# Projections spread over two bursts, and blocks that begin as soon as their tokens are split, in a two-layer attention kernel

## Chip, cores and metric

The kernel runs on one core of one Trainium2 chip. The metric is the device time of one execution in microseconds, the median of several runs.

## The reference

Four blocks run one after the other over 2048 tokens of width 576, in fp32: A, B, A, B, each on a layer norm of its input, each added to it. A is attention with 32 query heads of width 18 that share one key and one value head; B is linear attention with learned features. Both layers use the same weights.

```python
def _A_ref(x, wq, wk, wv, wo):
    q = (x @ wq).reshape(B, S, H, Dh).transpose(0, 2, 1, 3)
    k, v = x @ wk, x @ wv
    scores = jnp.einsum("bhqd,bkd->bhqk", q, k) * (Dh ** -0.5)
    o = jnp.einsum("bhqk,bkd->bhqd", _softmax(scores), v)
    return o.transpose(0, 2, 1, 3).reshape(B, S, H * Dh) @ wo

def _B_ref(x, wqkv, w_phi, wo):
    q, k, v = ...            # x @ wqkv, by heads
    pq = jnp.einsum("bhsd,hdf->bhsf", q, w_phi)      # pk likewise from k
    phi_q = concat([_softmax(pq), _softmax(-pq)])    # phi_k likewise
    kv = jnp.einsum("bhsf,bhsd->bhfd", phi_k, v)
    z = jnp.einsum("bhsf->bhf", phi_k)
    o = (phi_q @ kv) / (phi_q @ z + 1e-6)
    return o.transpose(0, 2, 1, 3).reshape(B, S, D) @ wo

x = x + _A_ref(_layernorm(x), ...)
x = x + _B_ref(_layernorm(x), ...)
# and both once more
```

## The kernel before

A layer here is A followed by B. Nearly all its time goes to one loop in `attend`, which computes A's attention and, in the gaps, most of B's projections for those token tiles whose attention is already finished. There are 16 token tiles of 128 tokens. A group is one token tile with half of the heads, so there are 32 groups; a unit is one group, one key tile and half of the group's heads, so a loop has 1024 units.

For each unit TensorE (PE) makes two score products into one of three score tiles `sc` (line 572), ScalarE (ACT) takes their exponential into a tile `pt` (line 1044), and PE later adds both units of a key tile into the group's sums, four products per key tile (line 850; "a key tile of sums" below). The sums of a group stand in one of two banks of PSUM, `acc` and `ps`, which change roles from group to group; the bank that is free takes the projections. When a group's last key tile is added, `finish_group` turns, divides and splits its sums on VectorE (DVE) and writes them to DRAM.

The loop goes in bursts of `BURST` = 3 units (`burst`). A burst issues the scores of three units and then does one of two things. Either it fills the free bank with one bankful of projections (`fill`), 14 products of 288 columns (`project`, line 257); or it adds key tiles of sums, two or three (`count`), and may add a state update (`U`, line 649) after them. A bankful costs one credit; `earn` gives `st["pace"]` credits per three units, and a burst with a bankful is followed by one without (`paused`). Where the side work has nothing to do (`st["idle"]`), two units and one key tile go at a time.

The side work is the generator `stream`. For each token tile it makes the output projection of finished attention (`output`, two bankfuls with the weights `wd`) and a block `mix`: keys (two bankfuls, `wa`), values (two, `wb`), queries (two, `wc`) and the state update. DVE takes each bankful out of PSUM (copies at lines 605 and 636) and makes the features. Eight bankfuls and one update go with each token tile, that is with 64 units.

The next tile's tokens are made ready beside that: layer norm in place on DVE (line 711), a block transpose on DVE (line 700), a write to DRAM (`flipped`, line 705) and a load back, turned (`xn`, lines 718 and 720); `turn_tokens` then splits them into high and low parts `xs` (lines 134, 135, 726, 727) once the previous block's update is issued. `turn_next` is asked after each bankful of a block: once it makes the statistics, the next time the turning. A block begins when `wanted` says so.

PE and DVE instructions of the loop are held in the order in which this code writes them (`in_order`), so what is written before what decides who waits.

Of the kernel before, what the change touches and what calls it, by code (L numbers as in the profile page):

```python
# [19 lines left out]
P = 128  # L20
# [4 lines left out]
NT = S // P  # L25
# [32 lines left out]
def traced(nc):  # L58
    return nc.cur_bb.bb.instructions
# [3 lines left out]
def kernel(ctx, tc, x_in, wq, wk, wv, wo, wqkv, w_phi, wob, out):  # L63
# [87 lines left out]
    def weight_tiles(place):  # L151
        hi = wpool.tile([P, KT, D], F32R, name=f"w{place}hi")
        return hi, (Parts("wclo") if place == "c" else wpool.tile([P, KT, D], F32R, name=f"w{place}lo"))
# [405 lines left out]
    def load_shifts(dst, layer, c, g):  # L559
        for j in range(2):  # L560
            src = mxds[layer][:, g * HG + j * HG // 2 : g * HG + (j + 1) * HG // 2, tokens(c)]
            to = dst[j * ROWT + KEYS : j * ROWT + STK].bitcast(F32)
            nc.sync.dma_start(to.rearrange("r p (x t) -> r (p x) t", t=P), src)
# [360 lines left out]
    def attend(layer, st, a1o, stream):  # L924
# [7 lines left out]
        def fetch(n):  # L932
            c, g = groups[n]
            qst[c, g] = a1.tile([P, 2, CW], F32R, name="qst")
            load_queries(qst[c, g], layer, c, g)
            load_shifts(qst[c, g], layer, c, g)

        with ctx1:
# [53 lines left out]
            def tick():  # L992
                ticks[0] += 1
                for queue in (urgent, loads, slow):
                    begun = len(traced(nc))
                    if queue and next(queue[0], DONE) is DONE:
                        queue.popleft()
                    if queue is loads:
                        for i in traced(nc)[begun:]:
                            if i.engine == mybir.EngineType.SP:  # L1000
                                tc.add_manual_dep(i, last[PE], SYNC if loads_at[0] is None else NOSYNC, reason="order")
                                loads_at[0] = i.name

            kind, credit, paused = [None], [0.0], [False]

            def peek():
                while kind[0] is None and bulk:
                    v = next(bulk[0], DONE)
                    if v is DONE:
                        bulk.popleft()  # L1010
                    elif v is STAGE:
                        break
                    elif isinstance(v, Kind):
                        kind[0] = v
                return kind[0]

            def fill():
                kind[0] = None
                while True:
                    v = next(bulk[0])  # L1020
                    assert v is not STAGE
                    if v < 0:
                        break
                in_order()

            last = {}

            def in_order():
                for i in traced(nc)[mark[0] :]:
                    if i.engine in PINNED:  # L1030
                        if i.engine in last:
                            tc.add_manual_dep(i, last[i.engine], NOSYNC, reason="order")
                        last[i.engine] = i.name
                mark[0] = len(traced(nc))
# [3 lines left out]
            pts, at, done = {}, [0], [0]  # L1038

            def expose(n, t, hh, pt):  # L1040
                sc = pss.tile([P, 2, 512], F32, name="sc")
                for j in range(2):
                    score(sc[:, j, :], qst[groups[n]], 2 * hh + j, t)
                A.activation(pt, sc, AF.Exp, scale=SCALE)  # L1044
                pts[n, t, hh] = pt

            spots = [*st["head"], *(a1.tile([P, 2, 512], F32, name="pt", bufs=TILES) for _ in range(2 * BURST))]
            acc[groups[0]] = bank(*homes[0], [P, CW])
            at[0] = len(spots)
            done[0] = (at[0] - 2 * BURST) // 2  # L1050

            def head_values(t, first, last):
                add_values(acc[groups[0]], t, [pts[0, t, j // 2][:, j % 2, :] for j in range(GH)], first, last)

            def head():
                for n, (unit, pt) in enumerate(zip(units, spots)):
                    expose(*unit, pt)
                    t = n // 2 - BURST
                    if n % 2 and t >= 0:
                        head_values(t, t == 0, False)  # L1060
# [6 lines left out]
            with tc.If(nc.values_load(safe[0:1, 0:1], min_val=0, max_val=1) == 0):  # L1067
# [5 lines left out]
                for g in range(2):  # L1073
                    load_shifts(st[f"q{g}"], layer, 0, g)
                head_values(BURST - 1, False, True)
                head()
# [6 lines left out]
            def scores(count):  # L1083
                ready = at[0] // 2
                for n, t, hh in units[at[0] : at[0] + count]:
                    if t == 0 and hh == 0 and 0 < n < len(groups) - 1:
                        fetch(n + 1)
                    expose(n, t, hh, a1.tile([P, 2, 512], F32, name="pt", bufs=TILES))
                    at[0] += 1
                in_order()  # L1090
                return ready

            def sums(until):
                while done[0] < until:
                    n, t, _ = units[2 * done[0]]
                    values(*groups[n], t, [pts.pop((n, t, hh)) for hh in range(2)])
                    done[0] += 1
                    in_order()

            def earn(count):  # L1100
                credit[0] = min(credit[0] + st["pace"] * count / BURST, 2)

            def burst():
                ready = scores(BURST)
                tick()
                earn(BURST)
                work = peek()
                held = at[0] + BURST - 2 * done[0]
                if work == "P" and credit[0] >= 1 and not paused[0] and held <= TILES:
                    fill()  # L1110
                    credit[0] -= 1
                    paused[0] = True
                else:
                    paused[0] = False
                    count = 3 if credit[0] + st["pace"] >= 1 else 2
                    until = min(ready, max(done[0] + count, -(-(at[0] + BURST - TILES) // 2)))
                    opens = any(t % NT == 0 for t in range(done[0], until))
                    if work == "F" and credit[0] >= 1 and not opens:
                        fill()
                        credit[0] -= 1  # L1120
                    sums(until)
                    if work == "U":
                        fill()
                    tick()
# [17 lines left out]
                run(gen)  # L1142

    BURST = 3
    TILES = 9
    DUE = 9
    SPILL = 4
    SETTLE = 3
    PACES = ((0.6, 0.39), (0.39, 0.39))
    FLIP = 84  # L1150
    TAIL = 100
    KEPT = NT - 3
    PE = mybir.EngineType.PE
    PINNED = (PE, mybir.EngineType.DVE)
# [17 lines left out]
    st = {"late": [], "norms": const.tile([P, NT // PAIR], F32, name="norms"), "wq": weight_tiles("b")}  # L1172
# [8 lines left out]
    def bank(pool, tag, shape):  # L1181
        t = pool.tile([P, CW], F32, name=tag)[: shape[0]]
        if len(shape) == 2:
            return t[:, : shape[1]]
        return t[:, : shape[1] * shape[2]].rearrange("p (a b) -> p a b", b=shape[2])
# [89 lines left out]
    for layer in range(LAYERS):  # L1275
        last = layer == LAYERS - 1
        st.update(start_state(bw), added=set())
        with tc.tile_pool(name="a1o", bufs=2) as a1o:

            def load(key, place, *args, **kw):  # L1280
                st[key] = weight_tiles(place) if isinstance(place, str) else place.weights()
                yield from reload_weight(key) if key in wd else load_weight(st[key], *args, **kw)
# [7 lines left out]
            def stream(v, layer=layer):  # L1290
                ps, loads, slow, finished, ticks = v.ps, v.loads, v.slow, v.finished, v.ticks
                residual = x_in.rearrange("(i p) d -> i p d", p=P) if layer == 0 else xd
                held, spoiled = deque(maxlen=3), set()
                unflipped, st["left"] = deque(), list(range(NT))
                st["closed"], st["pace"] = -1, PACES[layer][0]

# [41 lines left out]
                else:  # L1338
                    loads.append(load_wv())
                    loads.append(load("wk", "a", scratch[1], slice(0, D), padded=True))  # L1340
                    loads.append(load("wpq", "c", scratch[0], slice(0, D), padded=True))
                st["pace"] = PACES[layer][1]
                fetched = xs = None
                weights = False

                settled = 0
# [6 lines left out]
                        settled = v.left() - SETTLE  # L1353

                def wanted():
                    return (xs is not None and xs[0] != KEPT and v.left() <= settled
                            and (xs[0] < st["closed"] or xs[0] == NT - 2 or v.left() < TAIL))

                def flip(i, stats):
                    nonlocal fetched  # L1360
# [28 lines left out]
                while v.left():  # L1389
# [21 lines left out]
                    elif wanted():  # L1411
# [4 lines left out]
                        xs = None  # L1416
# [11 lines left out]

            st["heads_in"] = lambda: a1o.tile([P, 9, P], F32R, name="on", bufs=1)
            attend(layer, st, a1o, stream)  # L1430

            psx = ExitStack()
# [8 lines left out]
            with tc.tile_pool(name=f"tail{layer}", bufs=1) as tail:  # L1441
# [11 lines left out]
                xs = bw.tile([P, 9, P], F32R, name="xs2")  # L1453
# [115 lines left out]
```

## Time and profile before

| | |
|---|---|
| runs, us | 2678.7, 2674.51, 2678.91 (median 2678.7) |
| profiled execution, us | 2673.21 |
| its span, us | 2671.4 |
| mean granted PE clock | 0.993 |
| busy in the span: PE, DVE, ACT | 97%, 47%, 81% |

The span of an execution runs from its first to its last instruction. In a stretch of a timeline or a table, times are microseconds from the span's start; "PEld" is PE's load of weights, which runs beside its products. A row of the timeline gives start, length, engine, line, operation, output and inputs, the count, and in brackets how long the engine was idle before and who ended that. A table by stretch gives its bounds and length, the busy time of each engine with its count of instructions, the granted clock, the busy share of the DMA engines and GB/s. Products of fp32 sums (line 850) count twice in the profile, 24 rows for three key tiles.

### The profile page before, as it was taken

Reading aid. Unit: us, or ns where it says so; the run is one execution under the profiler, and the core shown is the slowest. Engines: PE = TensorE matmul, PEld = TensorE weight load, DVE = VectorE, ACT = ScalarE, POOL = GpSimd, SP = SyncE. Lnnn points to the kernel's source line nnn. Section 1 sums busy time; section 2 is a strip of 40 time slices with the busy share of each in tenths; the row PEclk is TensorE's granted clock in tenths of the full one; section 3 lists DMA queues with packets and bytes.
Section 4 is the critical chain, followed back from the end, with each engine's and each line's share of the span. In section 5 each row is a group of like instructions: output and inputs, shape, how many; then the busy total and the mean of one; then the engine's idle time right before and its main releaser. Section 6 shows DMA issues by size and latency. Waiting matters only on the chain. (4 is left out here: it accounts for less than half of the span.)

```text
span 2671.4 us, 55505 instructions
## 1 busy us (share of the span) xinstructions
PE 2597.6 (97%) x22002; PEld 1439.7 (54%) x22002; DVE 1266.8 (47%) x2871; ACT 2154.2 (81%) x2529; POOL 66.0 (2%) x106
## 2 busy tenths in 40 slices
PE   7989999999999999999999999999999999999999
PEld 6633444444444444438996344444444444444498
DVE  8444455444444444436774424444444444444265
ACT  4578989999999999994334999999999999999821
POOL 1000000000000000002000000000000000000010
PEclk9999999999999999999999999999999999999999
DMA  5465243222222222225643322222222222222164
GB/s 185 141 158 150 73 132 95 60 60 60 60 60 59 55 56 57 59 66 159 187 153 111 99 55 55 60 60 60 60 60 60 60 60 59 54 55 56 47 195 141
DMA packets 491633, 232.95 MB, mean 87 GB/s; under 512 B 237734, under 2 KB 458214, under 8 KB 491366
## 3 DMA queue, kind: packets, MB, share of 16 engines
q1 hardware_dynamic: 489894, 226.37, 31.4%
q8 instruction: 176, 2.88, 0.5%
q10 hardware_dynamic: 1472, 2.95, 0.4%
q14 instruction: 91, 0.75, 0.1%
HBM read 130.62 MB, written 96.67 MB: 85 GB/s over the span
## 5 line engine op out<-in xcount | busy, mean ns | idle before, releaser
L1044 ACT ACTIVATE pt<-sc 128x1024 f32<-128x1024 f32 x2036 | 1923.2, 1054 | 180.6 <-PE sc L572 158.9
L572 PE MATMUL sc<-qst,kst 56*128 56x512 f32 x3840 | 699.6, 452 | 22.5 <-ACT pt L1044 22.1
L572 PEld LDWEIGHTS sc<-qst,kst 56*128 56x128 f32 x3840 | 319.1, 184 | 564.8 <-ACT pt L1044 515.0
L850 PE MATMUL acc<-pt,vst 128*32 128x512 f32 x4096 | 500.3, 600 | 0.0
L850 PE MATMUL ps<-pt,vst 128*32 128x512 f32 x4048 | 480.9, 598 | 2.9 <-DVE featk L605 2.9
L850 PEld LDWEIGHTS ps<-pt,vst 128*32 128x32 f32 x4048 | 109.1, 109 | 229.2 <-issue 225.1
L850 PEld LDWEIGHTS acc<-pt,vst 128*32 128x32 f32 x4096 | 103.9, 109 | 211.0 <-issue 209.4
L321 DVE TENSOR_TENSOR xc<-xc,acc 128x288 f32<-128x288 f32 x60 | 27.2, 454 | 321.8 <-PE acc L257 321.8
L257 PE MATMUL ps<-wahi,xs 128*128 128x288 f32 x693 | 150.5, 303 | 2.1 <-ACT xs L132 1.9
L257 PE MATMUL ps<-wchi,xs 128*128 128x288 f32 x576 | 127.1, 306 | 0.0
L257 PE MATMUL acc<-wdhi,on 128*128 128x288 f32 x540 | 119.8, 307 | 3.2 <-DVE xc L321 3.2
L257 PEld LDWEIGHTS ps<-wahi,xs 128*128 128x128 f32 x693 | 114.4, 190 | 6.3 <-ACT xs L132 2.6
L257 PE MATMUL ps<-walo,xs 128*128 128x288 f32 x385 | 113.3, 297 | 0.0
L605 DVE COPY featk<-acc 128x288 f32<-128x288 f32 x51 | 23.3, 458 | 182.9 <-PE acc L257 182.9
L450 PE MATMUL ps<-xsc,wbhi 128*128 128x256 f32 x576 | 107.4, 285 | 0.6 <-ACT xsc L132 0.6
L472 ACT ACTIVATE pc<-ps 128x256 fp32r<-128x256 f32 x80 | 30.4, 384 | 93.2 <-PE ps L450 91.7
L257 PEld LDWEIGHTS ps<-wchi,xs 128*128 128x128 f32 x576 | 94.0, 188 | 19.2 <-issue 18.6
L132 ACT ACTIVATE xs<-ps 128x512 fp32r<-128x512 f32 x36 | 21.4, 595 | 102.7 <-PE ps L307 102.7
L257 PE MATMUL acc<-wahi,xs 128*128 128x288 f32 x459 | 101.8, 307 | 0.0
L257 PEld LDWEIGHTS acc<-wdhi,on 128*128 128x128 f32 x540 | 88.2, 188 | 24.9 <-issue 21.2
L257 PE MATMUL ps<-wclo,xs 128*128 128x288 f32 x320 | 94.2, 295 | 0.0
L450 PEld LDWEIGHTS ps<-xsc,wbhi 128*128 128x128 f32 x576 | 91.2, 193 | 1.6 <-ACT xsc L132 1.0
(256 smaller groups left out, 3064.4 us busy)
## 6 DMA issues: line engine op xcount, KB each, us to landing
qst<-qd SPq DMA_DIRECT2D x360, 72.0 KB
od<-parts SPq DMA_DIRECT2D x512, 36.0 KB
pht<-phi SPq DMA_DIRECT2D x32, 540.0 KB
qd<-pc SPq DMA_DIRECT2D x64, 256.0 KB
on<-od SPq DMA_DIRECT2D x60, 256.0 KB
phi<-pht SPq DMA_DIRECT2D x104, 144.0 KB
xd<-xc SPq DMA_DIRECT2D x33, 288.0 KB
flipped<-pht SPq DMA_DIRECT2D x112, 72.0 KB
```

The source lines that it names most:

```text
L132: A.activation(dst_hi, src, AF.Copy)
L257: T.matmul(dst, xs[:, slot, :], w[half][:, k, c0 : c0 + HALF], start=(n == 0), stop=(n == last))
L321: V.tensor_add(xr, xr, po)
L450: T.matmul(po, lhs, xsc[:, slot, :], start=(n == 0), stop=(n == LASTP))
L472: A.activation(pc[:, 0, :], po, AF.Copy)
L572: T.matmul(sc, kst[head_rows(h), t * P : (t + 1) * P], q[head_rows(h), h // 2, :], start=True, stop=True)
L605: V.tensor_copy(e[:, hs, 0, :], src)
L850: T.matmul(acc[32 * j : 32 * j + 32, :], vst[:, t, :], pts[j], start=first, stop=last)
L1044: A.activation(pt, sc, AF.Exp, scale=SCALE)
```

## The change

`fill` can run only a part of a bankful: `PIECE` = 3 steps, six products, and the rest (eight) in a later burst. With less than one credit but at least half of one, a burst begins a bankful and pays 0.5; the rest costs 0.5 too. Bursts with sums add three key tiles instead of two already from half a credit in sight. The pace becomes 0.38 instead of 0.39. `wanted` no longer asks that a later token tile's attention is closed, so a block may begin right after its tokens are split (three units after that is issued, `SETTLE`).

```diff
-            def fill():
-                kind[0] = None
-                while True:
+            def fill(steps=None):
+                while steps != 0:
                     v = next(bulk[0])
                     assert v is not STAGE
                     if v < 0:
+                        kind[0], begun[0] = None, False
                         break
+                    if steps is not None:
+                        steps -= 1
+                        begun[0] = True
                 in_order()
...
-                if work == "P" and credit[0] >= 1 and not paused[0] and held <= TILES:
-                    fill()
-                    credit[0] -= 1
+                whole = begun[0] or credit[0] >= 1
+                part = 0.5 if begun[0] or not whole else 1
+                opens = any(t % NT == 0 for t in range(done[0], done[0] + 4))
+                if (work == "P" and credit[0] >= part and not paused[0] and held <= TILES
+                        and (whole or not opens)):
+                    fill(None if whole else PIECE)
+                    credit[0] -= part
                     paused[0] = True
                 else:
                     paused[0] = False
-                    count = 3 if credit[0] + st["pace"] >= 1 else 2
+                    count = 3 if credit[0] + st["pace"] >= 0.5 else 2
...
+    PIECE = 3
...
-    PACES = ((0.6, 0.39), (0.39, 0.39))
+    PACES = ((0.6, 0.38), (0.38, 0.38))
     FLIP = 84
-    TAIL = 100
...
                 def wanted():
-                    return (xs is not None and xs[0] != KEPT and v.left() <= settled
-                            and (xs[0] < st["closed"] or xs[0] == NT - 2 or v.left() < TAIL))
+                    return xs is not None and xs[0] != KEPT and v.left() <= settled
```

More of the change, by code (lines that the diff above doesn't have):

```diff
@@ L1002, in tick @@
                                 loads_at[0] = i.name
-            kind, credit, paused = [None], [0.0], [False]
+            kind, credit, paused, begun = [None], [0.0], [False], [False]
             def peek():
```

## The prediction

> **What bounds the kernel now.** I read the page first, then busy time by stretch for the tile `pt` alone (the exponentials on ACT and the sums that read them), then the timeline of single bursts. The page:
>
> ```profile
> span 2671.4 us, 55505 instructions
> PE 2597.6 (97%) x22002; PEld 1439.7 (54%) x22002; DVE 1266.8 (47%) x2871; ACT 2154.2 (81%) x2529; POOL 66.0 (2%) x106
> ```
>
> PE looks full and ACT nearly so. The change touches the two attention loops only, so these are cut into stretches: both loops from the end of the first state update (line 649) to the end of the last, one token block, and the idle stretch at the end.
>
> ```profile
> 331.91:1149.11 817.20, 362.05 (x3048) 82.14 (x3048) 722.50 (x762) 1.00 0.27 67
> 1636.62:2456.81 820.19, 364.39 (x3072) 82.59 (x3072) 727.68 (x768) 1.00 0.24 58
> 739.27:807.59 68.32, 30.37 (x256) 6.88 (x256) 60.65 (x64) 1.00 0.24 58
> 807.59:817.05 9.46, 5.05 (x40) 0.89 (x40) 8.86 (x10) 1.00 0.17 50
> 846.62:855.26 8.64, 5.70 (x48) 1.25 (x48) 8.44 (x10) 1.00 0.14 39
> 2490.00:2510.00 20.00, 10.99 (x92) 1.57 (x80) 19.05 (x22) 1.00 0.21 58
> ```
>
> First the length, then PE, weight loads and ACT with counts, then the clock. One block takes 68.32 us for 64 exponentials. Without projections an exponential costs 20.00 / 22 = 0.91 us; three bursts with two key tiles of sums each take 8.64 us for nine (the tenth belongs to a neighbour), 0.96 each. A projection pair is dearer:
>
> ```profile
> 823.70 0.53 PEld L572 LDWEIGHTS sc<-qst,kst 56*128 56x128 f32 x6 [0.84 <-ACT pt L1044]
> 824.31 5.80 ACT L1044 ACTIVATE pt<-sc 128x1024 f32<-128x1024 f32 x6 [0.28 <-PE sc L572]
> 824.60 0.19 PEld L257 LDWEIGHTS acc<-wahi,xs 128*128 128x128 f32 x1 [0.36 <-issue]
> ...
> 826.65 0.30 PEld L572 LDWEIGHTS sc<-qst,kst 56*128 56x128 f32 x4 [0.16 <-issue]
> 827.22 0.19 PEld L572 LDWEIGHTS sc<-qst,kst 56*128 56x128 f32 x2 [0.27 <-ACT pt L1044]
> 827.64 2.78 PE L850 MATMUL ps<-pt,vst 128*32 128x512 f32 x24
> ...
> 830.35 0.53 PEld L572 LDWEIGHTS sc<-qst,kst 56*128 56x128 f32 x6 [0.84 <-ACT pt L1044]
> ```
>
> From 823.70 to 830.35 it is three scores, 14 products, three scores, three key tiles of sums: 6.65 us for six exponentials, 1.11 each. The row to see is 827.22: even behind all 14 products the sixth score waits, because there are three score tiles and the third exponential still holds one. The sums start 0.42 us after it and last 2.71 (to 830.35); meanwhile ACT has only three scores left and runs dry. So the long sums after a full burst set the pair's length, not the products.
>
> **The split bankful.** With six products instead of 14 (14 take 826.65 - 824.60 = 2.05; about 0.13 each) the second burst's scores reach PE 1.05 us earlier; with eight, 0.79 earlier. The first exponential starts 0.61 after the first score in both, so the third ends when it did, the sixth score goes at 827.22 as before and the sums at 827.64. The products saved become a wait on PE: a pair with 6, 8 or 14 products costs 6.65 us. That is an estimate for the new pairs, since no row has one; its floor is PE's own work, 5.60 and 5.86 us.
>
> The order shows what was traded. PE inside a block, before: three bursts with two key tiles each, between two bankfuls.
>
> ```order
> L572 MATMUL sc<-qst,kst 128x512 x6
> L850 MATMUL ps<-pt,vst 32x512 x8
> L572 MATMUL sc<-qst,kst 128x512 x6
> L850 MATMUL acc<-pt,vst 32x512 x8
> L572 MATMUL sc<-qst,kst 128x512 x6
> L850 MATMUL acc<-pt,vst 32x512 x8
> ```
>
> After, inside a block of layer 2:
>
> ```order
> L572 MATMUL sc<-qst,kst 128x512 x6
> L257 MATMUL ps<-wahi,xs 128x288
> L257 MATMUL ps<-walo,xs 128x288
> L257 MATMUL ps<-wahi,xs 128x288 x2
> L257 MATMUL ps<-walo,xs 128x288
> L257 MATMUL ps<-wahi,xs 128x288
> L572 MATMUL sc<-qst,kst 128x512 x6
> L850 MATMUL acc<-pt,vst 32x512 x12
> ```
>
> The cheap double-tile bursts are gone and triple sums, which need a pair each, stand in their place. Counted over both loops in PE's order: 47 bankfuls are split, bursts ending in triple sums rise from 186 to 263 (the new limit 0.5 for three), double ones fall from 129 to 38, and one-tile steps with two scores from 142 to 95.
>
> Blocks now come as 10 pairs and an update (60 exponentials), or these and one burst with one tile and one with two (66). The update costs 807.59 - 804.31 - 2.71 = 0.57:
>
> ```profile
> 804.31 2.78 PE L850 MATMUL acc<-pt,vst 128*32 128x512 f32 x24
> ...
> 807.59 0.53 PEld L572 LDWEIGHTS sc<-qst,kst 56*128 56x128 f32 x6
> ```
>
> The short pair I price from the 9.46 us row, six tenths, 5.7. So 60 cost 67.1 and 66 cost 72.8. Layer 1 has five and seven: 845.1 for 762, where the first row has 817.2 for 762: **+28**. Layer 2 has four and seven (778.0), and a block of 84 with nine pairs, an update and 30 exponentials at the idle price (87.7): 865.7 for 786. Before: 820.2 for 768, and 18 more in the idle stretch at 0.91: 836.6. **+29**. Together **+57 us**. No wall time comes from the earlier start by itself: exponentials are fixed in number, and the stretch moves to idle bursts.
>
> **Blocks that begin at once.** Before, DVE turned the next token tile (line 711) a projection pair and more ahead of the update; row 792.43 is such a place.
>
> ```profile
> 792.43 0.57 DVE L711 TENSOR_SCALAR xc<-xc,rstd,lnb 128x576 f32<-128x576 f32 x1
> 793.85 1.99 SPq L705 DMA_DIRECT2D flipped<-pht  x4
> 797.33 0.38 SPq L718 DMA_DIRECT2D xn<-flipped  x1
> ...
> 258.65 0.58 SPq L166 DMA_DIRECT2D wstage<-folded  x1
> 262.37 0.46 DVE L134 CAST wchi<-wstage 128x576 fp32r<-128x576 f32 x1 [2.00 <-DMA wstage<-folded]
> ```
>
> Turning goes out to DRAM and back: the load is issued 4.9 us after 792.43. Its landing has no row; it lies between its issue (4.9) and the 3.7 us from issue to use of the load at 258.65 (8.6). I take 7.3, since the stores needed about 1.5 us to land (797.33 - 795.84). DVE's order around the update, before (the turning stands 15 rows above):
>
> ```order
> L609 TENSOR_TENSOR featq<-fmin,featq 128x16x18
> L610 TENSOR_TENSOR featq<-featq,fmax 128x16x18
> L655 TENSOR_TENSOR kv<-kv,ps 128x288
> L134 CAST xs<-xn 128x512
> L135 TENSOR_TENSOR xs<-xn,xs 128x512
> ```
>
> After, in layer 2:
>
> ```order
> L610 TENSOR_TENSOR featq<-featq,fmax 128x16x18
> L711 TENSOR_SCALAR xc<-xc,rstd_21664,lnb_21666 128x576
> L700 STREAM_TRANSPOSE pht<-xc 128x576
> L655 TENSOR_TENSOR kv<-kv,ps 128x288
> L134 CAST xs<-xn 128x512
> L135 TENSOR_TENSOR xs<-xn,xs 128x512
> ```
>
> The turning has slid to right before the update, so the split behind it must wait for the round trip, and the next key projections for the split. Six blocks of layer 2 stand so.
>
> ```profile
> 805.25 0.46 DVE L610 TENSOR_TENSOR featq<-featq,fmax 128x288 f32<-128x288 f32 x1
> 808.07 0.42 DVE L134 CAST xs<-xn 128x512 fp32r<-128x512 f32 x1
> 808.52 0.69 DVE L135 TENSOR_TENSOR xs<-xn,xs 128x512 fp32r<-128x512 f32 x1
> ```
>
> In this block, turning at 805.7, behind line 610, would land at 813.0, 4.9 us after 808.07. Even undelayed the split ends at 809.2, 0.5 after the third product wants it (807.59 and 0.9 of scores and two products of 0.13): 5.4 us per block, less 1.05 in the three whose first burst has six products. **+29** (15 to 37 with the ends of the landing). Queued behind on DVE are the next copies out of PSUM; on PE everything.
>
> One block before already began straight after its update:
>
> ```profile
> 331.91 0.53 PEld L572 LDWEIGHTS sc<-qst,kst 56*128 56x128 f32 x6
> 335.41 0.54 PEld L572 LDWEIGHTS sc<-qst,kst 56*128 56x128 f32 x6 [0.16 <-ACT pt L1044]
> 339.24 2.55 PE L850 MATMUL ps<-pt,vst 128*32 128x512 f32 x16 [2.86 <-DVE featk L605]
> 345.38 0.53 PEld L572 LDWEIGHTS sc<-qst,kst 56*128 56x128 f32 x6 [0.84 <-ACT pt L1044]
> ...
> 338.00:341.00 3.00, 1.76 (x16) 0.42 (x16) 2.86 (x8) 0.88 (x1) 0.00 (x0) 0.90 0.32 76
> 341.00:344.00 3.00, 3.00 (x17) 1.04 (x17) 2.41 (x4) 2.06 (x3) 0.00 (x0) 0.53 0.17 64
> 344.00:348.00 4.00, 4.00 (x38) 1.13 (x30) 0.00 (x0) 3.48 (x5) 0.00 (x0) 1.00 0.91 261
> ```
>
> A new sum bank had to wait 2.86 us for DVE's copy, because the end of an attention group stands ahead of that copy in DVE's order. The three bursts took 13.5 us against 8.7 (826.65 - 823.70 and two double-tile bursts at 2.88), **4.8** lost. In two blocks of layer 1 DVE's order is the same: **+9.5**. Nine others only meet the 0.5 us of the split: **+5**.
>
> The last rows also show the clock: after the wait of 2.86 us it was 0.53 for 3 us (0.10 and 0.47 of 3 us lost, 1.7 us). Six longer waits cost six times that, **+10**. [...]
>
> Sum: 57 + 29 + 9.5 + 5 + 10 = **110.5 us**. The profiled execution took 2673.2 (span 2671.4), so 2783.7; it lay 5.5 below the median 2678.7 of the runs, so the forecast is **2789**.
>
> **Rivals.**
> *Cover holds.* The round trip and DVE's queue hide, only the pairs cost: 2678.7 + 57 = 2736. For it: DVE is busy 47%. Against: the order leaves no instruction between turning and split that lasts 5 us.
> *Faster.* If PE alone bounds, split pairs take 5.60 and 5.86: 47 x (1.05 + 0.79) = 86 saved, 57 - 86 = -29, and if the stalls hide too, 2650. It decides where a sixth score need not wait for ACT. For it: PE's 97%. Against: row 827.22. [...]
> *Clock in every pair.* If each of the 94 half-bankful pairs' waits of 0.8 to 1.05 us halved the clock as above, 94 x 1.7 = 160 more: 2949. Against: in the stretch 807.59:817.05, whose bursts wait for ACT on PE, the clock is 1.00. [...]
> *Nothing.* The products fall as ordered, so this needs gains and losses to cancel.
>
> **How the numbers follow.** Forecast case 0.70, cover 0.19, faster 0.05, clock 0.04, nothing 0.02. The range runs from 2728, the covered case with the split pairs 0.1 us cheaper (94 x 0.1 = 9), to 2823: landing at its far end (+8), all pairs 0.1 us dearer (263 x 0.1 = 26). Faster or slower means by over 0.2%, about what a measurement of this kernel can tell: 0.05, 0.02, 0.93.
>
> **What would show it.** Right: 6.65 us for pairs with 6 and 8 products, the wait in front of their sixth score; DVE waiting some 5 us for `xn<-flipped` in six blocks of layer 2, with the clock at half behind each. Wrong: pairs under 6.2 us, or `xs` split without a wait.

## The result and the profile after

| | before | after |
|---|---|---|
| median of the runs, us | 2676.61 (4 runs, 2673.64 to 2678.91) | 2809.24 (4 runs, 2807.66 to 2812.07) |
| profiled span, us | 2671.4 | 2805.9 |
| mean granted PE clock | 0.993 | 0.984 |

The changed kernel is slower: 1.0502 times the time before, 95% interval 1.0489 to 1.0515. The medians differ by 132.6 us, the two profiled spans by 134.5. Forecast were 2789 us and a range of 2728 to 2823.

The busy times of after, then three groups of instructions, each before and after (busy time and mean; then the idle time in front of the group and who ended most of it). Lines behind the change have moved by three: the exponential, 1044 before, is 1047.

```profile
PE 2636.1 (94%) x22002; PEld 1461.3 (52%) x22002; DVE 1261.4 (45%) x2871; ACT 2149.6 (77%) x2529; POOL 66.0 (2%) x106
...
L1044 ACT ACTIVATE pt<-sc 128x1024 f32<-128x1024 f32 x2036 | 1923.2, 1054 | 180.6 <-PE sc L572 158.9
L1047 ACT ACTIVATE pt<-sc 128x1024 f32<-128x1024 f32 x2036 | 1922.2, 1052 | 312.1 <-PE sc L572 298.2
L572 PE MATMUL sc<-qst,kst 56*128 56x512 f32 x3840 | 699.6, 452 | 22.5 <-ACT pt L1044 22.1
L572 PE MATMUL sc<-qst,kst 56*128 56x512 f32 x3840 | 717.8, 454 | 69.5 <-ACT pt L1047 69.3
L257 PE MATMUL ps<-wahi,xs 128*128 128x288 f32 x693 | 150.5, 303 | 2.1 <-ACT xs L132 1.9
L257 PE MATMUL ps<-wahi,xs 128*128 128x288 f32 x882 | 201.4, 313 | 41.5 <-DVE xs L134 38.0
```

PE and ACT issue as many instructions as before, and ACT is busy as long (2154.2 us before). What has grown is waiting. ACT was idle 312.1 us in front of its exponentials, most of it waiting for scores, where it was 180.6 before. PE's scores waited 69.5 us where it was 22.5, nearly all for an exponential: that is where the split pairs show. PE waited 38.0 us for the split of tokens, where it had no such wait: the blocks that begin at once.

By stretch, from the end of the first state update to the end of the last, for tile `pt` alone (length, PE, weight loads and ACT, clock):

```profile
330.10:1195.00 864.90, 358.79 (x3048) 85.46 (x3048) 721.78 (x762) 1.00 0.25 64
1671.70:2596.40 924.70, 371.67 (x3144) 87.86 (x3144) 744.27 (x786) 0.97 0.22 53
```

The counts are the forecast's, 762 and 786 exponentials. Layer 1 took 864.9 - 817.2 = 47.7 us longer. Layer 2 took 924.7 against the 836.6 worked out for before, 88.1 longer. Together that is 135.8, so all other parts of the kernel gave back 1.3.

**A split pair.** In the timeline of PE in layer 2, pairs with six, eight and 14 products follow each other (selected rows; a row is start, length, instruction and the idle time before it):

```profile
1706.24 0.53 PEld L572 LDWEIGHTS sc<-qst,kst 56*128 56x128 f32 x6 [0.84 <-ACT pt L1047]
1708.12 0.51 PE L572 MATMUL sc<-qst,kst 56*128 56x512 f32 x2
1708.84 0.49 PE L572 MATMUL sc<-qst,kst 56*128 56x512 f32 x2 [0.21 <-ACT pt L1047]
1709.75 0.51 PE L572 MATMUL sc<-qst,kst 56*128 56x512 f32 x2 [0.42 <-ACT pt L1047]
1710.19 2.78 PE L850 MATMUL ps<-pt,vst 128*32 128x512 f32 x24
...
1712.90 0.53 PEld L572 LDWEIGHTS sc<-qst,kst 56*128 56x128 f32 x6 [0.84 <-ACT pt L1047]
1716.41 0.50 PE L572 MATMUL sc<-qst,kst 56*128 56x512 f32 x2 [0.41 <-ACT pt L1047]
1716.84 2.78 PE L850 MATMUL ps<-pt,vst 128*32 128x512 f32 x24
...
1719.56 0.53 PEld L572 LDWEIGHTS sc<-qst,kst 56*128 56x128 f32 x6 [0.84 <-ACT pt L1047]
1723.07 0.19 PEld L572 LDWEIGHTS sc<-qst,kst 56*128 56x128 f32 x2 [0.27 <-ACT pt L1047]
1723.50 2.78 PE L850 MATMUL ps<-pt,vst 128*32 128x512 f32 x24
...
1726.21 0.53 PEld L572 LDWEIGHTS sc<-qst,kst 56*128 56x128 f32 x6 [0.84 <-ACT pt L1047]
```

The pairs begin at 1706.24, 1712.90, 1719.56 and the next at 1726.21: 6.66, 6.66 and 6.65 us, whatever the products. The sixth unit's scores (the prediction's "sixth score") stand at 1709.75, 1716.41 and 1723.07, each 3.51 us behind the pair's start. With six products PE had reached the fourth unit's already at 1708.12 and then waited for ACT before the fifth and again before the sixth.

**A block that begins at once.** The timeline around an update of layer 2, with SyncE's queue (SPq) and DVE, and then the one row of PE's waits that this fills (total, times, longest):

```profile
1906.77 0.58 DVE L711 TENSOR_SCALAR xc<-xc,rstd,lnb 128x576 f32<-128x576 f32 x1
1908.19 1.99 SPq L705 DMA_DIRECT2D flipped<-pht  x4
1908.73 0.53 PEld L572 LDWEIGHTS sc<-qst,kst 56*128 56x128 f32 x6
1911.78 0.38 SPq L718 DMA_DIRECT2D xn<-flipped  x1
1914.79 0.43 DVE L134 CAST xs<-xn 128x512 fp32r<-128x512 f32 x1 [5.50 <-DMA xn<-flipped]
1915.36 0.58 PE L257 MATMUL ps<-wahi,xs 128*128 128x288 f32 x1 [5.66 <-DVE xs L134]
...
PE ps L257 <- DVE xs L134: 38.0, 6, 8.0
```

The turning at 1906.77 comes back 8.02 us later, at 1914.79. The update is long done by then, its successor's first scores too, and PE waits 5.66 us at the first key projection. Six blocks do so.

The clock (seventh number, behind the five busy times) around that wait, and around the longest one:

```profile
1908.80:1912.20 3.40, 0.90 (x6) 0.41 (x6) 0.45 (x1) 2.85 (x3) 0.00 (x0) 1.00 0.70 132
1912.20:1919.03 6.83, 3.67 (x14) 3.40 (x14) 3.41 (x7) 0.00 (x0) 0.00 (x0) 0.50 0.22 69
1987.30:1997.54 10.24, 4.62 (x20) 2.70 (x24) 4.79 (x8) 2.67 (x4) 0.00 (x0) 0.50 0.35 84
```

It falls to half while PE is still waiting (1912.20) and stays there 3.7 us beyond the wait's end at 1915.36, so the products after the wait run slowly too: the one of `walo` and `xs` at 1915.74 took 0.44 us, the one at 1923.89, with the clock at 1.00 again, 0.29.

### The profile page after: what moved, and what is told of

The parts are those of the page before. It is cut to its first block, busy times and chain, and to the rows that moved or that the text cites. A ratio compares the mean times of both kernels' runs of the same rounds, so it can differ in the third digit from the quotient of the medians.

```text
span 2805.9 us, 55530 instructions
## 1 busy us (share of the span) xinstructions
PE 2636.1 (94%) x22002; PEld 1461.3 (52%) x22002; DVE 1261.4 (45%) x2871; ACT 2149.6 (77%) x2529; POOL 66.0 (2%) x106
## 5 line engine op out<-in xcount | busy, mean ns | idle before, releaser
L1047 ACT ACTIVATE pt<-sc 128x1024 f32<-128x1024 f32 x2036 | 1922.2, 1052 | 312.1 <-PE sc L572 298.2
L572 PE MATMUL sc<-qst,kst 56*128 56x512 f32 x3840 | 717.8, 454 | 69.5 <-ACT pt L1047 69.3
L572 PEld LDWEIGHTS sc<-qst,kst 56*128 56x128 f32 x3840 | 326.3, 185 | 573.8 <-ACT pt L1047 491.8
L850 PE MATMUL acc<-pt,vst 128*32 128x512 f32 x4096 | 493.1, 601 | 1.3 <-DVE vb L636 0.6
L850 PE MATMUL ps<-pt,vst 128*32 128x512 f32 x4048 | 487.2, 604 | 6.7 <-DVE featk L605 5.7
L257 PE MATMUL ps<-wahi,xs 128*128 128x288 f32 x882 | 201.4, 313 | 41.5 <-DVE xs L134 38.0
L850 PEld LDWEIGHTS ps<-pt,vst 128*32 128x32 f32 x4048 | 110.5, 110 | 242.0 <-issue 229.5
L257 PEld LDWEIGHTS ps<-wahi,xs 128*128 128x128 f32 x882 | 149.8, 195 | 58.6 <-issue 47.1
L257 PE MATMUL ps<-walo,xs 128*128 128x288 f32 x490 | 147.2, 303 | 0.0
L257 PE MATMUL ps<-wbhi,xs 128*128 128x288 f32 x423 | 93.9, 306 | 2.0 <-DVE turned L952 2.0
L257 PEld LDWEIGHTS ps<-walo,xs 128*128 128x128 f32 x490 | 95.7, 195 | 0.0
L605 DVE COPY featq<-ps 128x288 f32<-128x288 f32 x48 | 22.0, 458 | 157.0 <-PE ps L257 156.6
```

The costliest lines, as they stand in the source:

```text
L257: T.matmul(dst, xs[:, slot, :], w[half][:, k, c0 : c0 + HALF], start=(n == 0), stop=(n == last))
L572: T.matmul(sc, kst[head_rows(h), t * P : (t + 1) * P], q[head_rows(h), h // 2, :], start=True, stop=True)
L605: V.tensor_copy(e[:, hs, 0, :], src)
L850: T.matmul(acc[32 * j : 32 * j + 32, :], vst[:, t, :], pts[j], start=first, stop=last)
```

## The experiments

The runs were to tell three things apart: what the pairs cost and why, what the earlier start costs and why, and which piece of the change is worth keeping.

**e1: the change without the earlier start.**

```diff
+    TAIL = 100
...
 def wanted():
-    return xs is not None and xs[0] != KEPT and v.left() <= settled
+    return (xs is not None and xs[0] != KEPT and v.left() <= settled
+            and (xs[0] < st["closed"] or xs[0] == NT - 2 or v.left() < TAIL))
```

> The change without the earlier start of blocks (split bankfuls, the half-credit limit for triple sums and the pace stay). Counted in PE's order: 246 bursts with triple sums (186 before, 263 in the change), 42 double ones (129), 30 split bankfuls. Theory (a pair costs 6.65 us whatever its products; the round trip of the turned tokens is what the earlier start adds): about +50 us against before, 2727, ratio 1.019, no wait of DVE for xn<-flipped in blocks, clock at half nowhere inside the second loop. Rival (pairs with half a bankful cost less than 6.65, the loss is all in the start): 2676 or less, ratio 1.00. Rival (start harmless): 2809, ratio 1.05.

Measured: 2733.09 us (2727.98 to 2734.22), 1.0218 times before (1.0201 to 1.0235). No wait of PE for `xs` is left in layer 2. A block of 64 exponentials, by stretch:

```profile
1950.40:2020.30 69.90, 68.04 (x569) 33.56 (x560) 30.55 (x61) 62.75 (x68) 0.54 (x1) 1.00 0.24 57
```

It takes 69.9 us against 68.32 before, with the clock at 1.00. So the split bankfuls, with the limit and the pace, lose by themselves, without the earlier start and without a half clock. (One of the two openings of layer 1 is still there, a pair of 11.74 us at 549.5; so that opening doesn't hang on the earlier start.)

**e2: the earlier start alone.** The kernel before, with the new `wanted` of the change and nothing else.

> The kernel before with the earlier start alone (no split, old limits, old pace). PE's order has 159 triple bursts (186 before) and 186 double ones (129), so pairs alone would give -8 us. Six blocks begin behind a turning that stands right before their update. Theory: each of these loses 7 to 8 us (round trip plus half a clock window), 47 in all, less the 8: about 2715, ratio 1.015, and DVE waits of some 5 us for xn<-flipped. Rival (the round trip is covered by other work): 2668, ratio 0.997.

Measured: 2730.93 us (2727.28 to 2734.42), 1.0206 (1.0187 to 1.0225), some 16 us more than expected. The waits for the turned tokens, on DVE and on PE (total and times; for PE the longest too):

```profile
  DMA xn<-flipped: 65.9, 14
PE ps L257 <- DVE xs L134: 41.0, 9, 6.9
```

The round trip shows without any split bankful, in nine blocks instead of six. The pairs with a bankful are late by 76 us in all, against 10 before; the span grew by 60. So the earlier start, which in this kernel also leaves 27 triple sums fewer, gives back about 6 us and no more.

**e3: only the limit for triple sums.** The kernel before, with three key tiles from half a credit in sight.

```diff
-                    count = 3 if credit[0] + st["pace"] >= 1 else 2
+                    count = 3 if credit[0] + st["pace"] >= 0.5 else 2
```

> The kernel before with the limit for triple sums at 0.5 instead of 1, nothing else; no bankful is split. 216 triple bursts (186 before), 69 double ones (129), 142 single steps (142). Theory (the price is in the triple sums): +22 us, 2699, ratio 1.008; each new pair is 14 products and three key tiles at 6.65. Rival (only the half bankfuls cost): 2677, ratio 1.000.

Measured: 2693.5 us (2692.35 to 2694.72), 1.007 (1.0054 to 1.0087). A block:

```profile
743.77:812.83 69.06, 67.84 (x572) 33.37 (x561) 30.55 (x61) 62.86 (x68) 0.54 (x1) 1.00 0.24 58
```

It takes 69.06 us against 68.32, and no bankful is split here: more triple sums cost time even behind full bankfuls.

**e4: the change, with the split held back until the tokens are there.** The tokens are split at the earliest nine units after their turning was issued; the blocks may still begin early.

```diff
-                    if fetched is not None:
+                    if fetched is not None and v.left() <= fetched[2]:
                         xs = fetched[0], split_tokens(fetched[1])
...
-                    fetched = i, fetch_tokens(i)
+                    fetched = i, fetch_tokens(i), v.left() - 9
...
                     elif fetched is not None and xs is None:
-                        yield from rest(8)
+                        yield from wait(lambda: v.left() > fetched[2])
```

> The change, but a block's tokens are split only when nine units have passed since their turning was issued; otherwise the side work waits with idle bursts until then. Pairs nearly as in the change: 260 triple bursts, 39 double ones. Theory (six blocks of the second loop wait for the round trip): about 50 us of 2809 come back, 2757, ratio to before 1.030; no burst with a bankful over 6 us in the second loop. Rival (the wait is not the round trip but DVE's queue or PE's work): 2805, ratio 1.048.

Measured: 2753.01 us (2752.63 to 2757.19), 1.0297 (1.0279 to 1.0314), 56 us below the change. The second loop by stretch, from the end of its first update to the end of its last:

```profile
1670.86:2535.90 865.04, 833.23 (x6798) 409.46 (x6792) 365.15 (x732) 763.44 (x828) 6.49 (x12) 1.00 0.23 56
```

The clock is 1.00 throughout, where it was 0.97. Both openings of layer 1 remain, pairs of 11.75 and 11.74 us. With the wait gone its half clock is gone too, so the half clock hangs on the wait.

**e5 and e6: half of each exponential, in the change and in the kernel before.** ACT takes 512 of 1024 columns, and the sums read these twice. PE's work is unchanged.

```diff
-                add_values(acc[c, g], t, [pt[j // 2][:, j % 2, :] for j in range(GH)], t == 0, t == NT - 1)
+                add_values(acc[c, g], t, [pt[j // 2][:, 0, :] for j in range(GH)], t == 0, t == NT - 1)
...
-                A.activation(pt, sc, AF.Exp, scale=SCALE)
+                A.activation(pt[:, 0, :], sc[:, 0, :], AF.Exp, scale=SCALE)
...
-                add_values(acc[groups[0]], t, [pts[0, t, j // 2][:, j % 2, :] for j in range(GH)], first, last)
+                add_values(acc[groups[0]], t, [pts[0, t, j // 2][:, 0, :] for j in range(GH)], first, last)
```

> The change with half of each exponential left out: ACT takes only the first of a unit's two heads (512 of 1024 columns), and the sums read that half for both heads; the output is not the reference's. Theory (a split pair waits for the third exponential, which frees the score tile): the wait in front of the sixth score goes, pairs with 6 and 8 products fall to PE's own 5.6 and 5.9 us, pairs with 14 stay at 6.6. Rival (the pair's length is set by DVE's copies, the bank or PE itself): split pairs stay at 6.65. Total about 2690.

> The kernel before with the same half of the exponentials left out. Theory: with ACT out of the way the loop is bound by PE, single steps fall from 1.83 to about 1.6 and double bursts from 2.88 to 2.80; total about 2630, so the change's loss shrinks from 133 us to about 60, what the round trips, the openings and the splits of tokens cost (47, 15 and 5).

Measured in one run each: 2662.72 us (change) and 2578.42 us (before), 27 and 52 us under what was expected. Two split pairs of e5, six products and eight:

```profile
541.77 0.53 PEld L572 LDWEIGHTS sc<-qst,kst 56*128 56x128 f32 x6 [0.84 <-issue]
543.66 0.54 PEld L572 LDWEIGHTS sc<-qst,kst 56*128 56x128 f32 x6 [0.16 <-ACT pt L1047]
544.56 2.78 PE L850 MATMUL ps<-pt,vst 128*32 128x512 f32 x24
547.27 0.53 PEld L572 LDWEIGHTS sc<-qst,kst 56*128 56x128 f32 x6 [0.84 <-issue]
549.42 0.53 PEld L572 LDWEIGHTS sc<-qst,kst 56*128 56x128 f32 x6 [0.17 <-issue]
...
553.03 0.53 PEld L572 LDWEIGHTS sc<-qst,kst 56*128 56x128 f32 x6 [0.84 <-ACT featk L612]
```

They take 547.27 - 541.77 = 5.50 us and 5.76, against 6.65: the prediction's floors, 5.60 and 5.86, less 0.1. All three scores of the second burst go in one piece, so it was ACT's holding of the score tiles that made the split pairs as long as the full ones. A full pair, with 14 products, falls only from 6.66 to 6.56 us: there PE's own work is nearly as long as ACT's hold. The two kernels still differ by 84 us where the expectation had about 60: the waits for the tokens do not shrink with ACT's work. Measured against the usual length of their kind, the pairs of e5 are late by 88.6 us in all and those of e6 by 6.1, which is 82.5 of the 84. So 76 more pairs with a triple sum cost next to nothing once ACT's work is halved. The six blocks of layer 2 lie 53.5 us above their pairs' length here (46.9 in the change).

**e7 and e8: the limit the other way, and the pace alone.** The kernel before, with three key tiles only from 1.1 credits in sight (e7), or with the change's pace 0.38 (e8).

```diff
-                    count = 3 if credit[0] + st["pace"] >= 1 else 2
+                    count = 3 if credit[0] + st["pace"] >= 1.1 else 2
```

> The kernel before with the limit for triple sums raised from 1 to 1.1, nothing else: the opposite way. In PE's order triple bursts fall further and double ones rise. Theory (each traded pair is dearer than double bursts): about -16 us, 2660, ratio 0.994. Rival (the present limit is the best balance, PE binds either way): 2676, ratio 1.000.

> The kernel before with the pace 0.38 instead of 0.39, nothing else: the change's pace by itself. Theory: fewer credits in hand mean fewer triple sums; about -13 us, 2663, ratio 0.995. Rival (the pace only shifts work along the loop): 2676, ratio 1.000.

Measured: e7 2654.18 us (2650.97 to 2658.48), 0.9924 (0.9908 to 0.994); e8 2660.93 us (2659.66 to 2663.31), 0.995 (0.9936 to 0.9965). Both are faster than before; e7 beats both kernels of this case. One block of each, e7 first:

```profile
803.10:870.60 67.50, 67.10 (x572) 33.14 (x560) 30.56 (x61) 62.95 (x70) 0.55 (x1) 1.00 0.24 59
872.40:939.90 67.50, 67.10 (x561) 33.15 (x560) 30.55 (x61) 62.93 (x69) 0.54 (x1) 1.00 0.24 59
```

**What the runs say together.** The table counts, in PE's rows over the whole kernel, the pairs of a bankful, whole or part, with a triple sum behind it. Stalls are how far all pairs with a bankful lie above their usual length: 6.65 us with a triple sum (7.22 with an update), 5.79 with a double one (6.36). The last column is the span's change without the change in stalls, by the change in pairs:

| kernel | pairs | stalls, us | span, us | us for each pair more or less |
|---|---|---|---|---|
| before | 186 | 9.9 | 2671.4 | |
| e8 pace | 160 | 16.3 | 2659.3 | 0.72 |
| e7 limit 1.1 | 163 | 9.1 | 2652.9 | 0.77 |
| e3 limit 0.5 | 215 | 8.7 | 2690.6 | 0.70 |
| e1 without early start | 245 | 17.1 | 2726.2 | 0.81 |
| e4 split held back | 259 | 27.9 | 2750.9 | 0.84 |
| after | 262 | 80.1 | 2805.9 | 0.85 |
| e2 early start alone | 159 | 76.4 | 2731.4 | 0.24 |

For after it is (134.5 - 70.2) / 76. In both directions, with split bankfuls or without, each such pair costs 0.7 to 0.85 us, but not in e2: there 27 pairs fewer should give back some 20 us and gave about 6. Its blocks also begin at other times, and what takes the rest was not separated. So the price is an account that fits six kernels of seven; only e5 against e6 tells where it comes from.

## Why the prediction was right, and where it was short

| term | predicted, us | in the trace, us |
|---|---|---|
| pairs, layer 1 and layer 2 | 28 + 29 | 28.9 + 32.5 |
| wait for the round trip, six blocks | 29 | 34.8 |
| half clock behind it | 10 | 12.1 |
| two openings in layer 1 | 9.5 | 10.2 |
| nine token splits | 5 | 4.0 |
| not foreseen: two openings in layer 2 | 0 | 5.2 |
| not foreseen: the first blocks of layer 1 | 0 | 4.4 |
| small waits in other pairs | 0 | 3.7 |
| outside the loops | 0 | -1.3 |
| sum | 110.5 | 134.5 |

In this table a stall is what a pair with a triple sum, inside the two loops, takes above 6.65 us (7.22 with an update), less the same of before: 74.4 us in all. The pairs' own price is what is left of 47.7 and 88.1, so it holds whatever else changed there. The measured 134.5 are 24 us more than the sum, and no large miss hides another: all but two of the terms came out as forecast or dearer.

**The split pair** was right in mechanism and in size. It was an estimate with no row behind it; the three rows now give 6.65 to 6.66, and e5 shows that the price goes when ACT's work is halved. That the sums "set the pair's length, not the products" holds for the split pairs alone: for a full pair e5 has PE's own work at 6.56 us, 0.1 under the pair. The rival "faster", which priced these pairs at 5.60 and 5.86, holds in e5 and not in the change: it decides on who is late at the sixth score, as it said.

**The round trip** was right in place and kind, with a mis-sized landing. The first and the fifth of the six turnings, and where DVE got their tokens:

```profile
1669.75 0.58 DVE L711 TENSOR_SCALAR xc<-xc,rstd,lnb 128x576 f32<-128x576 f32 x1
1679.07 0.43 DVE L134 CAST xs<-xn 128x512 fp32r<-128x512 f32 x1 [6.79 <-DMA xn<-flipped]
...
1984.60 0.57 DVE L711 TENSOR_SCALAR xc<-xc,rstd,lnb 128x576 f32<-128x576 f32 x1
1992.35 0.43 DVE L134 CAST xs<-xn 128x512 fp32r<-128x512 f32 x1 [6.02 <-DMA xn<-flipped]
```

That is 9.32 and 7.75 us, the longest and the shortest; the mean of all six is 8.26 where 7.3 was taken (the bounds were 4.9 and 8.6, and the longest lies beyond them). Six times 0.96 is 5.8, the whole miss of this term. From the sum of waits, 38.0, three times the credit of 1.05 us for blocks that start with six products is taken to get 34.8. The rows bear the credit out: pairs with six products lie on average 1.02 us further above their usual length than PE waited in them, pairs with 14 products 1.96. The extra 2.1 us of half clock are mis-sized too: its price had been read off a stretch behind a wait of 2.86 us, where the clock was 0.53 over 3 us. Behind these longer waits it was at 0.50 for 6.83 us, and once for 10.24, as the rows by stretch above show. No run shows the "clock window" of which e2's expectation puts half behind each wait; these stretches at 0.50 are what after shows there. (12.1 is what is left of the six blocks' 46.9 when the 34.8 are taken off; it was not measured by itself.)

That wait and clock belong together and lie there, e4 shows: 56 us go, of which the six blocks are 46.9 and the two openings of layer 2, gone as well, 5.2. The rival "cover holds" falls with that, and "clock in every pair" with the pairs of e1, whose block ran at 1.00.

**The openings** went as read from before. One in layer 1, on DVE and PE:

```profile
549.17 0.53 PEld L572 LDWEIGHTS sc<-qst,kst 56*128 56x128 f32 x6
553.55 0.69 DVE L135 TENSOR_TENSOR parts<-osb,parts 128x512 fp32r<-128x512 f32 x1
556.00 0.45 DVE L605 COPY featk<-ps 128x288 f32<-128x288 f32 x1
556.50 4.48 PE L850 MATMUL ps<-pt,vst 128*32 128x512 f32 x24 [2.86 <-DVE featk L605]
...
560.91 0.53 PEld L572 LDWEIGHTS sc<-qst,kst 56*128 56x128 f32 x6 [1.35 <-issue]
```

The end of the attention group (last at 553.55) stands on DVE ahead of the copy that frees the bank, and the sums wait 2.86 us, to the hundredth as before: 11.74 us instead of 6.65. It isn't alone there: DVE is busy without a gap from the split of the tokens (549.70) to the copy, with 1.6 us of split, 2.9 of the group's end and 1.9 of features. **What was overlooked:** the prediction looked at this order only where the sums wait. In two blocks of layer 2 the same DVE work makes ACT late instead, one pair further on:

```profile
2317.87 1.03 ACT L1047 ACTIVATE pt<-sc 128x1024 f32<-128x1024 f32 x1 [0.76 <-PE sc L572]
...
2319.28 0.69 ACT L612 ACTIVATE featk<-featk 128x576 f32<-128x576 f32 x1 [0.39 <-DVE featk L610]
2319.87 4.66 ACT L1047 ACTIVATE pt<-sc 128x1024 f32<-128x1024 f32 x5
2320.93 0.49 PE L572 MATMUL sc<-qst,kst 56*128 56x512 f32 x2 [1.27 <-ACT pt L1047]
```

The exponential of the features (line 612) stands in ACT's order between two of the attention's and waits for DVE; the second exponential starts at 2319.87, a microsecond after the first ended, and PE stands behind it. The first blocks of layer 1 (4.4 us) were not looked at in the order at all; what makes each of them late I have not separated. That DVE's group end is the cause of the openings is read from the rows and was not tried by moving it.

**No gain from the earlier start by itself**, the prediction said; e2, with nothing else changed, is 55 us above before, and 76 us separate e1 from the whole change. The 76 include more triple-sum pairs (17 between e1 and after, 14 us at 0.85), which the prediction had in its term for the pairs.

## What to carry to other kernels

Where a few buffers between two engines are the limit, work moved out of a burst only buys time if the burst's last buffer is free by then: find the instruction that waits for it (here the sixth unit's scores, 3.51 us behind the pair's start whatever the products) before counting saved products. Price a unit of the schedule, here a pair with a triple sum at 0.7 to 0.85 us, and count it, but look for the kernel where the price fails (here e2); then try the count in both directions, since the kernel before was not at its best either. Before letting work begin "as soon as it is issued", look up in the trace how long its data is on the way, and what all engines, not only the first one that waits, have queued behind it.

## What the hardware showed unexpectedly

The half clock came in steps. In the loops of after it lasted 3.41 us with PE's waits of 2.85 and 2.86 us, 6.83 us with the five of 5.66 to 6.96 us, and 10.24 us with the one of 7.97 us: one, two and three times 3.41. Its ten starts there lie whole numbers of that step apart: 1676.70, 1758.62 and 1833.71, for instance, are 24 and 22 steps apart. It did not take one long wait. In the second pair of an opening in layer 2 PE's longest is 1.27 us (row 2320.93). Two stretches of 3.4 us there, the lower clock in the second, and one of a split pair:

```profile
2318.40:2321.80 3.40, 1.75 (x10) 0.96 (x9) 2.10 (x3) 3.02 (x5) 0.00 (x0) 1.00 0.16 31
2321.80:2325.20 3.40, 3.36 (x18) 0.95 (x22) 0.00 (x0) 2.73 (x3) 0.00 (x0) 0.50 0.82 208
...
1708.10:1711.50 3.40, 2.77 (x20) 0.97 (x22) 0.00 (x0) 3.40 (x5) 0.00 (x0) 1.00 0.54 154
```

With PE busy for 1.75 of 3.40 us the next stretch ran at half clock; with 2.77 of 3.40, in split pairs, the clock stayed. Where it turned can be counted in the traces of before and after, cut into such steps of 3.41 us from the starts of the half clock, over all steps at full clock from where their record of the clock begins (16.1 us and 14.4 us). All 16 with PE busy for under 1.5 us were followed by one at half clock, and none with more than 2.05 us was. Of the eleven in between six were and five were not, so PE's busy time alone does not decide it there. What makes the steps 3.41 us long, no run shows.
